# Clusters of 64-wide TensorE work, one pool of PSUM banks, a contiguous q/k copy and weights in pieces, in a fused attention and FFN kernel

## The chip, the cores and the metric

The kernel runs on one core of one Trainium2 chip. The metric is the device time of one execution in microseconds (us), as the median of several runs. A profile is one execution taken with the hardware profiler, so its span differs a little from the median. TensorE appears in the profile as PE (matmuls) and PEld (weight loads), VectorE as DVE, ScalarE as ACT, GpSimd as POOL, SyncE as SP. In this kernel SBUF holds the operands, and TensorE's results go to PSUM, which the program divides into 8 banks, and are copied out from there.

## The reference, cut to what matters

```python
# B=8, heads H=12, S=448, D=64;  F = H*D = 768, FF = 2048
scores = scale * q @ k.T
scores = einsum('bhij,hg->bgij', scores, w_pre)      # mixes the heads
attn   = softmax(scores)
attn   = einsum('bhij,hg->bgij', attn, w_post)       # mixes the heads again
x      = (attn @ v) as [B*S, F]
out    = relu(x @ w_in)**2 @ w_out
```

## The kernel before

The program is written as a list of tasks with dependencies. TensorE runs its tasks in the order in which they are listed. A small planner orders the tasks of the other engines by start time and then by priority (a lower number goes first), and gives each copy out of PSUM to ACT or DVE. So the order of everything is fixed before the run.

One batch has these parts. I use the names in the rest of the text:

- T: transposes of q and k, one pair of heads at a time, into one PSUM bank; copied to SBUF.
- QK: scores of a pair of heads, two matmuls with 64 contraction rows that run side by side in the two row halves of the array; copied into `stage`.
- A DMA on the SP queue copies 10 query rows x 12 heads from `stage` into `dring`, so that heads lie on partitions. This is one *chunk*; a batch has 45.
- pre (head mix by w_pre), exp on ACT, then post (head mix by w_post, 4 matmuls), then a copy into `a2t`.
- AV: attention times v, 64 output columns a head, so two heads side by side in the column halves of the array. It runs once for the first part of a batch's chunks and once for the rest.
- F1 and F2: the two FFN products, with the square (`h2t`) on POOL.

T and AV use the array as two 128x64 halves, QK as two 64x128 halves, the rest as one 128x128 array.

```python
# four fixed pairs of banks: scores, pre, post, everything else
psA = pp("psA", [128, 2, 512], DT.float32)
psP = pp("psP", [128, 2, 512], DT.float32)
psQ = pp("psQ", [128, 2, 512], DT.float32)
psF = pp("psF", [128, 2, 512], DT.float32)
...
def emit_T(b, p):                       # one pair of heads, one task
    ... 16 transposes into one psF bank ...
    def fn_q(eng, en, p=p, pb=pb, bank=bank):          # q: written with a stride
        o = qtp[:, pb, p, :].rearrange("d (j r) -> d r j", r=RJ)
        i_ = psF_bf[:, bank, 0:S].rearrange("d (r j) -> d r j", r=RJ)
        return copy(eng, en, o, i_)
    def fn_k(...): return copy(eng, en, ktp[:, pb, p, :], psF_bf[:, bank, S:2 * S])
    tk = add(..., [t_tr, tq] + war, ...)               # k waits for q
...
def emit_load_w():                      # two loads, each a whole weight
    last["w_in"]  = plan.add("ldwin",  POOL, fn_in,  [qk_tasks[(0, H - 1)]], ..., -300.0, ...)
    last["w_out"] = plan.add("ldwout", POOL, fn_out, [qk_tasks[(0, H - 1)]], ..., -299.0, ...)
# q and k of batch b: priority b * 1000.0 - 500.0
...
head = weave(units_AV(b - 1, 1), late_f2, 2)   # AV units one by one, between other work
body = weave(f1, units_T(b + 1), 2)            # so are the T units
```

The softmax here doesn't subtract the row's maximum and nothing guards it: scores larger than these inputs give would overflow.

Of the kernel before, what the change touches and what calls it, by code (L numbers as in the profile page):

```python
# [8 lines left out]
DT = mybir.dt  # L9
# [8 lines left out]
SEM_LAT = 60.0  # L18
ACT_BIAS = 50.0
# [11 lines left out]
class _Task:  # L31
# [4 lines left out]
                 "end", "order", "nwait", "succs", "clock", "avail")  # L36

    def __init__(self, name, engine, fn, deps, cost, prio, sem, seminc):
        self.name = name
        self.engine = engine  # L40
        self.fn = fn
        self.deps = []
        for d in deps:
            if d is not None and d not in self.deps:
                self.deps.append(d)
        self.cost = cost
        self.prio = prio
        self.sem = sem
        self.seminc = seminc
        self.semval = 0  # L50
        self.end = None
        self.clock = None


class _Plan:
# [11 lines left out]
    def schedule(self):  # L67
# [11 lines left out]
        npe = 0  # L79
        ready = [t for t in self.tasks if t.nwait == 0 and t.engine != PE]  # L80
        while len(committed) < len(self.tasks):
# [16 lines left out]
            if e == PE:  # L98
                npe += 1
            else:  # L100
                ready.remove(t)
# [15 lines left out]
def bass_talking_heads_attention__then__ffn_squared_relu_kernel(  # L117
# [25 lines left out]
    HC = (26, NCH - 26)  # L143
# [4 lines left out]
    with ExitStack() as es:  # L148
# [10 lines left out]
        NH1 = 3  # L159
        ident = sb("ident", [128, 128], DT.bfloat16)  # L160
# [12 lines left out]
        qtp = sb("qtp", [128, 2, NP, S], DT.bfloat16)  # L173
        ktp = sb("ktp", [128, 2, NP, S], DT.bfloat16)
# [9 lines left out]
        psA = pp("psA", [128, 2, 512], DT.float32)  # L184
        psP = pp("psP", [128, 2, 512], DT.float32)
        psQ = pp("psQ", [128, 2, 512], DT.float32)
        psF = pp("psF", [128, 2, 512], DT.float32)
        psF_bf = psF.bitcast(DT.bfloat16)
# [7 lines left out]
        sem_qk = [Sm("dqk%d" % i) for i in range(6)]  # L196
        sem_v = Sm("dv")
        sem_w = [Sm("dwin"), Sm("dwout")]
# [15 lines left out]
        def add(name, engine, fn, deps, cost, prio):  # L214
            return plan.add(name, engine, fn, deps, cost, prio, "ctr", 1)
# [7 lines left out]
        def fn_init(eng, en):  # L223
            eng.memset(ident[:, :], 0.0)
            eng.memset(mask[:, :], 1.0)
            return eng.memset(pring[:, :, S:S + 16], 0.0)

        t_init = add("init", POOL, fn_init, [], {POOL: (800.0, 900.0)}, -1e6)

        def fn_init2(eng, en):  # L230
            eng.affine_select(ident[:, :], ident[:, :], pattern=[[-1, 128]],
                              compare_op=ALU.not_equal, fill=1.0, base=0,
                              channel_multiplier=1)
# [4 lines left out]
        t_init2 = add("init2", POOL, fn_init2, [t_init], {POOL: (800.0, 900.0)}, -1e6 + 1)  # L238

        def fn_init3(eng, en):  # L240
# [4 lines left out]
        t_init3 = add("init3", POOL, fn_init3, [t_init2], {POOL: (400.0, 500.0)}, -1e6 + 2)  # L245
# [16 lines left out]
        t_wk1 = add("wk1", DVE, fn_wk1, [t_wsmall, t_init3], {DVE: (300.0, 400.0)}, -1e6)  # L262
# [7 lines left out]
        t_wk2 = add("wk2", DVE, fn_wk2, [t_wsmall, t_init3], {DVE: (300.0, 400.0)}, -1e6 + 1)  # L270
# [7 lines left out]
        def emit_load_qk(b):  # L278
            step = 2 if b == 0 else H
            for h0 in range(0, H, step):  # L280
                sem = sem_qk[h0 // step]

                def fn(eng, en, b=b, h0=h0, step=step, sem=sem):
# [6 lines left out]
                             {POOL: (2000.0, 5000.0 if b == 0 else 9000.0)}, b * 1000.0 - 500.0, sem, 32)  # L290
# [3 lines left out]
        def emit_load_v(b):  # L294
            def fn(eng, en, b=b):
# [4 lines left out]
                                 {POOL: (1200.0, 8000.0)}, b * 1000.0 - 400.0, sem_v, 16)  # L300

        def emit_load_w():
            def fn_in(eng, en):
                src = bass.AP(moe_w_in.tensor, 0, [[FF, 128], [128 * FF, NFT], [1, FF]])
                eng.dma_start(w_in_sb[:, :, :], src).then_inc(sem_w[0].handle, 16)

            def fn_out(eng, en):
                src = bass.AP(moe_w_out.tensor, 0, [[F, 128], [128 * F, NFFT], [1, F]])
                eng.dma_start(w_out_sb[:, :, :], src).then_inc(sem_w[1].handle, 16)

            last["w_in"] = plan.add("ldwin", POOL, fn_in, [qk_tasks[(0, H - 1)]],
                                    {POOL: (1200.0, 25000.0)}, -300.0, sem_w[0], 16)
            last["w_out"] = plan.add("ldwout", POOL, fn_out, [qk_tasks[(0, H - 1)]],
                                     {POOL: (1200.0, 45000.0)}, -299.0, sem_w[1], 16)


        fbank = {"n": 0, 0: [], 1: []}

        def take_bank():
            i = fbank["n"] % 2  # L320
            fbank["n"] += 1
            return i, fbank[i]
# [4 lines left out]
        def emit_T(b, p):  # L327
            pb = b % 2
            bank, freed = take_bank()

            def fn_tr(eng, en, p=p, bank=bank):
                r_ = None
                for i, src in enumerate((qraw, kraw)):
                    for r in range(RJ):
                        for kk in range(2):
                            r_ = eng.transpose(  # L336
                                psF_bf[kk * 64:kk * 64 + 64, bank,
                                       i * S + r * JB:i * S + (r + 1) * JB],
                                src[:, 2 * p + kk, r, :],
                                ident[0:JB, 0:JB],  # L340
                            )
                return r_

            t_tr = add("tr%d_%d" % (b, p), PE, fn_tr,
                       [qk_tasks[(b, 2 * p)], qk_tasks[(b, 2 * p + 1)], t_init2] + freed,
                       c_mm(2 * RJ, JB, 20.0), 0)
            last["T"] = t_tr

            def fn_q(eng, en, p=p, pb=pb, bank=bank):
                o = qtp[:, pb, p, :].rearrange("d (j r) -> d r j", r=RJ)  # L350
                i_ = psF_bf[:, bank, 0:S].rearrange("d (r j) -> d r j", r=RJ)
                return copy(eng, en, o, i_)

            def fn_k(eng, en, p=p, pb=pb, bank=bank):
                return copy(eng, en, ktp[:, pb, p, :], psF_bf[:, bank, S:2 * S])

            war = [last.get(("qk", b - 2))]
            tq = add("tq%d_%d" % (b, p), FLEX, fn_q, [t_tr] + war, c_ev(S), b * 1000.0 - 700)
            tk = add("tk%d_%d" % (b, p), FLEX, fn_k, [t_tr, tq] + war, c_ev(S),
                     b * 1000.0 - 699)  # L360
            trev[(b, p)] = [tq, tk]
            fbank[bank] = [tq, tk]
# [3 lines left out]
        psA_free = []  # L366

        def emit_QK(b, T, p):
            pb = b % 2
            nr = min(IT, S - T * IT)  # L370
            sl = (b * NIT + T) % 2

            def fn_qk(eng, en, T=T, p=p, pb=pb, nr=nr):
                r_ = None
                for par in range(2):
                    r0 = par * 64
                    r_ = eng.matmul(  # L377
                        psA[0:nr, par, 0:S],
                        qtp[r0:r0 + 64, pb, p, T * IT:T * IT + nr],
                        ktp[r0:r0 + 64, pb, p, 0:S],  # L380
                        start=True, stop=True,
                    )
                return r_

            t_qk = add("qk%d_%d_%d" % (b, T, p), PE, fn_qk, trev[(b, p)] + psA_free,
                       c_mm(1, S, 8.0), 0)
            last[("qk", b)] = t_qk

            def fn_sev(eng, en, p=p, sl=sl, nr=nr):
                return copy(eng, en, stage[0:nr, sl, 2 * p:2 * p + 2, :], psA[0:nr, 0:2, 0:S])  # L390

            t_sev = add("sev%d_%d_%d" % (b, T, p), FLEX, fn_sev,
                        [t_qk] + stage_reader.get(sl, []), c_ev(2 * S),
                        b * 1000.0 + 20 + 10 * T)
            psA_free[:] = [t_sev]
            sev.setdefault((b, T), []).append(t_sev)
            if p == NP - 1:
# [8 lines left out]
        def emit_rel(b, T, u, sl):  # L406
# [5 lines left out]
            def fn(eng, en, u=u, nv=nv, sl=sl, slot=slot):  # L412
# [6 lines left out]
                         {SP: (1200.0, 3200.0)}, g * 1.0, sem_dsl[slot], 16)  # L419
# [19 lines left out]
        def emit_pre(g):  # L439
            b, c = divmod(g, NCH)  # L440
            slot, bank, ps = g % NDS, g % 2, g % NPS

            def fn_pre(eng, en, slot=slot, bank=bank):
                return eng.matmul(psP[0:NR, bank, 0:S], wk1[:, :, :], dring[:, slot, :],  # L444
                                  start=True, stop=True)

            t_pre = add("pre%d_%d" % (b, c), PE, fn_pre,
                        [rel[g], t_wk1, exp_of.get(g - 2)], c_mm(1, S), 0)
# [4 lines left out]
            def fn_exp(eng, en, ps=ps, bank=bank):  # L453
                return eng.activation(pring[:, ps, 0:S], psP[0:NR, bank, 0:S], AF.Exp,  # L454
                                      accum_out=rowsum[:, ps, :])
# [4 lines left out]
            exp_of[g] = t_exp  # L460

            def fn_rec(eng, en, ps=ps):
                return eng.reciprocal(rinv[:, ps, :], rowsum[:, ps, :])  # L463
# [4 lines left out]
            def fn_fold(eng, en, ps=ps, ws=g % NWS):  # L468
# [440 lines left out]
```

## Time and profile before

The median of the first three runs was 715.93 us, and the profiled execution spans 718.5 us.

| what | value | view |
|---|---|---|
| PE busy | 629.5 us, 88% | page, part 1 |
| chain of waits through PE / DMA | 81% / 7% | page, part 4 |
| first post of batch 1 | 144.5 us | timeline |
| batches 2 to 6, first post to first post | 79.9 and 74.1 us in turn, mean 77.6 | timeline |
| PE idle before T of batch 1 | 21.3 us | waits |

The page of the kernel before, its busy shares and two rows of its 40 slices of 18 us (a digit is tenths busy):

```profile
PE 629.5 (88%) x5576; PEld 368.6 (51%) x5576; DVE 380.7 (53%) x946; ACT 488.9 (68%) x1129; POOL 287.0 (40%) x566
PE   3314779987889999999999999999999999999996
PEclk9999799998999999999999999999999999999999
```

There are two stages. For about the first 145 us PE is often idle; after that it is nearly always busy. They have to be read apart.

Waits of PE in the first 146 us of the kernel before (who waited for whom: us in total, times, longest):

```profile
PE psF L336 <- DMA kraw<-in_k_dram: 26.9, 2, 21.3
PE psP L444 <- DMA dring<-stage: 13.0, 7, 5.9
PE psA L377 <- ACT ktp L219: 10.9, 6, 1.8
PE psA L377 <- ACT stage L219: 7.9, 6, 3.0
```

L336 is T, L444 pre, L377 QK. The largest single wait is T of batch 1, which waits for its k. In the timeline of the kernel before it stands in front of all other work of PE:

```profile
41.13 0.63 PE L444 MATMUL psP<-dring,wk 120*120 120x448 bf16 x1 [0.92 <-DMA dring<-stage]
63.08 0.59 PE L336 MATMUL psF<-ident,qraw 112*64 112x112 bf16 x8 [21.32 <-DMA kraw<-in_k_dram]
```

The steady stage of the kernel before, in two batches (window, its length, then busy time of each engine, granted clock, DMA share, GB/s):

```profile
208.00:288.00 80.00, 78.24 (x691) 44.12 (x687) 45.54 (x110) 62.27 (x142) 36.16 (x68) 1.00 0.52 105
288.00:362.00 74.00, 73.89 (x669) 41.52 (x665) 45.37 (x111) 60.61 (x140) 36.15 (x68) 1.00 0.57 109
```

The columns after the length are PE, PEld, DVE, ACT and POOL. PE is busy about 98% of the time or more, so nothing but less PE time helps here. Part of that busy time is not streaming, though. PE's timeline of the kernel before (start, length, instruction, count):

```profile
308.17 0.74 PE L562 MATMUL psF<-xt,w_in_sb 128*128 128x448 bf16 x3
308.84 0.40 PE L377 MATMUL psA<-ktp,qtp 64*120 64x448 bf16 x2
309.17 0.38 PE L489 MATMUL psQ<-wk2s,pring 120*128 120x120 bf16 x4
309.39 0.35 PE L444 MATMUL psP<-dring,wk 120*120 120x448 bf16 x1
309.59 0.73 PE L562 MATMUL psF<-xt,w_in_sb 128*128 128x448 bf16 x3
310.16 0.37 PE L489 MATMUL psQ<-wk2s,pring 120*128 120x120 bf16 x4
310.46 0.39 PE L336 MATMUL psF<-ident,qraw 112*64 112x112 bf16 x8
```

Read the differences of starts, not the lengths, because matmuls overlap. The three F1 matmuls at 309.59 take 0.57 us until the next start, 0.19 each. But the three at 308.17 take 0.67 us, because QK follows them, and the pair of QK takes 0.33 us until post starts, although its 448 columns stream in about 0.19. Over a window of 400 us the medians are 189 ns from F1 to F1, 281 from F1 to QK, and 329 from the last QK matmul to post. I call such a detour to 64-wide work and back an *excursion*. The Trainium skill, "TensorEngine Tiling (Array Packing)", section Tiling Modes (Key Properties), says that a change of tiling mode drains the TensorE. The gaps in this trace fit that (a drain itself is not to be seen in it), and they give the price: one QK pair costs 92 + 3 + 329 = 424 ns, about 235 more than it streams.

### The profile page before, as it was taken

The page shows a single profiled execution, that of the slowest core. Times are in us where ns is not written, and L with a number is a line of the kernel's source. Part 1 is how long each engine was busy: PE and PEld are TensorE (multiplying, and loading weights), DVE is VectorE, ACT ScalarE, POOL GpSimd, SP SyncE. Part 2 cuts the span into 40 slices and gives each one's busy share as a digit, 9 for nine tenths or more (in the row PEclk, how much of TensorE's full clock was granted, in tenths as well). Part 3 has the DMA queues.
Part 4 walks back from the last instruction along what each step waited for, and adds up shares of the span by engine and source line. Part 5 has one row for each costly group of instructions (what it writes and reads, how often), then busy time and mean ns, then how long its engine had stood idle before and what let it go on. Part 6 is the DMA issues. An engine that isn't in the chain of part 4 may idle for free.

```text
span 718.5 us, 14744 instructions
## 1 busy us (share of the span) xinstructions
PE 629.5 (88%) x5576; PEld 368.6 (51%) x5576; DVE 380.7 (53%) x946; ACT 488.9 (68%) x1129; POOL 287.0 (40%) x566
## 2 busy tenths in 40 slices
PE   3314779987889999999999999999999999999996
PEld 1103346554555555555555455555555455557663
DVE  1112564776765645577556455575556554436442
ACT  4314660897878967788778867887788676866510
POOL 6100325343525632357236622565246423742200
PEclk9999799998999999999999999999999999999999
DMA  9994841274656473467445824638463234533011
GB/s 115 215 223 63 131 103 32 61 150 103 100 104 133 80 147 81 110 112 113 106 110 106 135 62 114 130 77 131 117 121 85 54 90 94 97 87 77 23 45 45
DMA packets 84873, 73.32 MB, mean 102 GB/s; under 512 B 4932, under 2 KB 82244, under 8 KB 84804
## 3 DMA queue, kind: packets, MB, share of 16 engines
q0 software_dynamic: 37952, 33.82, 27.1%
q1 hardware_dynamic: 46852, 38.56, 24.0%
q8 instruction: 45, 0.74, 0.4%
q14 instruction: 24, 0.20, 0.1%
HBM read 45.62 MB, written 11.01 MB: 79 GB/s over the span
## 4 chain that ended last, share of the span: by engine, by line
PE 81%; DMA 7%; ACT 4%; DVE 4%; POOL 2%; issue 1%; SPq 0%; POOLq 0%
PE psF L625 21%; PE psF L562 20%; PE psQ L489 13%; PE psP L444 9%; PE psA L377 9%; PE psF L521 6%; DMA kraw<-in_k_dram 6%; PE psF L336 4%; DMA dring<-stage 2%; ACT pring L454 1%; DVE a2t L220 1%; ACT stage L219 1%; POOL h2t L597 1%; DVE qtp L220 1%; ACT a2t L219 1%
## 5 line engine op out<-in xcount | busy, mean ns | idle before, releaser
L469 POOL TENSOR_SCALAR wk2s<-wk2b,rinv 120x120 bf16<-120x120 bf16 x360 | 131.0, 365 | 305.2 <-DVE rinv L463 302.3
L454 ACT ACTIVATE pring<-psP 120x448 bf16<-120x448 f32 x360 | 196.1, 546 | 67.3 <-PE psP L444 65.9
L220 DVE CAST a2t<-psQ 112x480 bf16<-112x480 f32 x221 | 144.5, 656 | 99.5 <-PE psQ L489 95.6
L562 PE MATMUL psF<-xt,w_in_sb 128*128 128x448 bf16 (+2 forms) x960 | 187.0, 316 | 5.1 <-DVE ktp L220 3.2
L625 PE MATMUL psF<-w_out_sb,h2t 128*128 128x384 bf16 x896 | 177.2, 325 | 9.0 <-POOL h2t L597 7.4
L219 ACT ACTIVATE stage<-psA 120x896 bf16<-120x896 f32 (+1 forms) x147 | 134.6, 916 | 60.5 <-PE psA L377 57.4
L444 PE MATMUL psP<-dring,wk 120*120 120x448 bf16 x360 | 135.2, 376 | 14.4 <-DMA dring<-stage 13.0
L489 PE MATMUL psQ<-wk2s,pring 120*128 120x120 bf16 x1440 | 140.5, 221 | 0.1
L489 PEld LDWEIGHTS psQ<-wk2s,pring 120*128 120x128 bf16 x1440 | 93.2, 99 | 63.1 <-issue 25.2
L597 POOL TENSOR_TENSOR h2t<-h1t 128x448 bf16<-128x448 bf16 (+2 forms) x128 | 107.3, 839 | 37.0 <-DVE h1t L588 17.6
L625 PEld LDWEIGHTS psF<-w_out_sb,h2t 128*128 128x128 bf16 x896 | 82.0, 98 | 54.1 <-POOL h2t L597 9.3
L562 PEld LDWEIGHTS psF<-xt,w_in_sb 128*128 128x128 bf16 x960 | 84.1, 99 | 47.8 <-DVE ktp L220 5.6
L463 DVE RECIPROCAL rinv<-rowsum 120x1 f32<-120x1 f32 x360 | 56.6, 158 | 90.6 <-ACT pring L454 87.9
L377 PE MATMUL psA<-ktp,qtp 64*120 64x448 bf16 (+1 forms) x384 | 80.5, 416 | 26.3 <-ACT stage L219 13.6
L219 ACT ACTIVATE a2t<-psQ 112x480 bf16<-112x480 f32 x139 | 80.0, 575 | 28.8 <-PE psQ L489 24.9
L454 ACT ACTIVATION_READ_ACCUMULATOR pring<-psP 120x1 f32 x360 | 71.4, 198 | 0.0
L444 PEld LDWEIGHTS psP<-dring,wk 120*120 120x120 bf16 x360 | 49.1, 136 | 39.8 <-DMA dring<-stage 14.0
L377 PEld LDWEIGHTS psA<-ktp,qtp 64*120 64x120 bf16 (+1 forms) x384 | 25.0, 127 | 81.8 <-issue 32.0
L220 DVE CAST stage<-psA 120x896 bf16<-120x896 f32 (+1 forms) x45 | 49.0, 1090 | 29.4 <-PE psA L377 28.1
L521 PE MATMUL psF<-a2t,vraw 112*64 112x260 bf16 (+1 forms) x768 | 53.5, 264 | 1.7 <-DVE a2t L220 0.7
L220 DVE COPY osb<-psF 128x384 f32<-128x384 f32 x54 | 30.1, 557 | 42.0 <-PE psF L625 42.0
L588 DVE TENSOR_SCALAR h1t<-psF 128x448 bf16<-128x448 f32 (+2 forms) x89 | 43.8, 492 | 10.6 <-PE psF L562 9.0
(33 smaller groups left out, 314.1 us busy)
## 6 DMA issues: line engine op xcount, KB each, us to landing
dring<-stage SPq DMA_DIRECT2D x352, 105.0 KB
out_dram<-osb POOLq DMA_DIRECT2D x24, 384.0 KB, 4.5
vraw<-in_v_dram POOLq DMA_DIRECT2D x8, 672.0 KB, 12.3
qraw<-in_q_dram POOLq DMA_DIRECT2D x7, 672.0 KB, 8.5
kraw<-in_k_dram POOLq DMA_DIRECT2D x7, 672.0 KB, 14.2
w_in_sb<-in_moe_w_in_dram POOLq DMA_DIRECT2D x1, 3072.0 KB, 20.9
w_out_sb<-in_moe_w_out_dram POOLq DMA_DIRECT2D x1, 3072.0 KB, 40.6
out_dram<-osb POOLq DMA_DIRECT2D x8, 192.0 KB, 3.8
```

The source lines that it names most:

```text
L219: return eng.activation(o, i_, AF.Copy)
L220: return eng.tensor_copy(o, i_)
L377: r_ = eng.matmul(psA[0:nr, par, 0:S], qtp[r0:r0 + 64, pb, p, T * IT:T * IT + nr], ktp[r0:r0 + 64, pb, p, 0:S], start=True, stop=True,)
L444: return eng.matmul(psP[0:NR, bank, 0:S], wk1[:, :, :], dring[:, slot, :], start=True, stop=True)
L454: return eng.activation(pring[:, ps, 0:S], psP[0:NR, bank, 0:S], AF.Exp, accum_out=rowsum[:, ps, :])
L463: return eng.reciprocal(rinv[:, ps, :], rowsum[:, ps, :])
L469: return eng.tensor_scalar(wk2s[:, ws, :], wk2b[:, :, :].rearrange("p a b -> p (a b)"), rinv[:, ps, :], 1.0, op0=ALU.mult, op1=ALU.mult)
L489: r_ = eng.matmul(psQ[0:128, bank, jb * NR:(jb + 1) * NR], pring[:, ps, jb * JB:jb * JB + 128], wk2s[:, ws, :], start=True, stop=True,)
L521: r_ = eng.matmul(psF[kk * 64:kk * 64 + 64, bank, 0:n], vraw[:, 2 * p + kk, r, :], a2t[half][:, r, 2 * p + kk, 0:n], start=(r == 0), stop= ...
L562: r_ = eng.matmul(psF[:, bank, 0:n], w_in_sb[:, ft, t16 * 128:(t16 + 1) * 128], xt[:, ft, c0:c1], start=(ft == 0), stop=(ft == NFT - 1),)
L597: return eng.tensor_tensor(h2t[:, t16, o0:o0 + n], h1t[:, s, 0:n], h1t[:, s, 0:n], ALU.mult)
L625: r_ = eng.matmul(psF[:, bank, 0:FH], h2t[:, t16, col:col + 128], w_out_sb[:, t16, hh * FH:(hh + 1) * FH], start=(t16 == 0), stop=(t16 == ...
```

## The change

The intent is to make fewer excursions by running QK in clusters of two pairs, T in clusters of three and AV of a half batch as one cluster. Clusters need more PSUM banks at one time, so all 8 banks become one pool. Further parts: the rows of q and k stay in the order in which they were loaded, so that the copy is contiguous and does q and k together (the output rows are put right by the output DMA, now two DMAs for most tiles); two head pairs of AV share a bank, which limits a half batch to 256 columns and moves the split from 26 chunks to 23; AV goes between F1 and F2; the weights come in 8 pieces, those of w_in in rows of 512 columns; and T of batch 1 is held back to chunks 14 and 18 of batch 0. Smaller parts are not in the cut below, among them: q and k of batch 0 come in three loads instead of six, the later scores of batch 0 are listed three chunks later, and the planner reckons 100 ns for a change of the tile size. In the diffs, `...` marks a cut, and some lines tell an edit in words or shortened.

```diff
-    HC = (26, NCH - 26)
+    HC = (23, NCH - 23)
-        psA = pp("psA", [128, 2, 512], DT.float32)     # and psP, psQ, psF
+        ps = pp("ps", [128, 8, 512], DT.float32)
+        def take(n=1):                                 # the n adjacent banks free longest
+            runs = [list(range(i, i + n)) for i in range(NB - n + 1)]
+            runs = [r_ for r_ in runs if all(i in bank_age for i in r_)]
+            got = min(runs, key=lambda r_: max(bank_age.index(i) for i in r_))
...
-            def fn_q(...): ...                         # strided
-            def fn_k(...): ...
+                def fn_ev(eng, en, p=p, pb=pb, bank=bank):
+                    return copy(eng, en, qkt[:, pb, p, :, :], ps_bf[:, bank, 0:2 * S])
...
+        NWP = 4
-            last["w_in"] = plan.add("ldwin", POOL, fn_in, [qk_tasks[(0, H - 1)]], ..., -300.0, ...)
+                last["w%d_%d" % (i, j)] = plan.add("ldw%d_%d" % (i, j), POOL, fn, [],
+                    ..., -1400.0 + 300.0 * i + j, sem_w[i][j], 16)
-    # q and k of batch b: b * 1000.0 - 500.0
+    # q and k of batch b: -1e7 + h0 if b == 0 else b * 1000.0 - 1500.0
...
-            return [[(..., (lambda p=p: emit_T(b, p)))] for p in range(NP)]
+            return [Group([(..., (lambda p=p: emit_T(b, (p, p + 1, p + 2))))], "T", sl)
+                    for p, sl in zip((0, 3), slots)]
-            body = weave(f1, ts, 2)
+                ts = units_T(b + 1, (14, 18)) if b == 0 else units_T(b + 1)
+            body = weave(f1, ts, 5)
+        NQ = 2                                         # pairs of heads in a QK cluster
+                at = max([0] + [i + 1 for i, g in enumerate(queue) if g.kind == "F1"])
+                queue[at:at] = [g for g in tail if g.kind == "AV"]     # between F1 and F2
```

## The prediction

> **What bounds the kernel now.** The page's busy row gives PE 88% of the span, ACT 68%, DVE 53%; the chain of waits runs 81% through PE and 7% through DMA. Two different stages:
>
> - Start. In the timeline PE idles 21.3 us (41.8 to 63.1) before the transposes of batch 1: their q and k were issued at 23.5 us but stand in the same DMA queue behind the two weight loads, issued at 14.0 and 14.8 us. Only four pre-mix products run before 63 us. The six transpose/score rounds of batch 0 take 3.3 us each because the two copies of q (1.15 us) and k (0.4 to 0.5 us) run one after the other through two banks. Batch 1's first post-mix starts at 144.5 us, of which I count some 63 us as PE work.
> - Steady state (208 to 596 us, five batches of 77.6 us). The windows view has PE busy 78.3 of 80 us, ACT 62, DVE 46: PE bound. Part is not streaming. Start-to-start in PE's timeline: an F1 matmul takes 189 ns before another F1 but 281 before a score pair (+92); pre 193, but 284 before transposes or AV (+91); a score pair occupies 329 ns before post instead of about 190 (+139); leaving AV or transposes costs about 95. The Trainium skill, "TensorEngine Tiling (Array Packing)", Key Properties, says a change of tiling mode drains the TensorE; these gaps agree.
>
> **What the change does.**
> 1. Clusters: a batch has 24 score, 12 AV and 6 transpose excursions; after it 12, 2 and 2. At 231, 187 and 187 ns: 8.9 us before, 3.5 after: 5.4 us a batch, on the critical path. Over the seven PE-bound batches about 37 us.
> 2. AV goes between F1 and F2: hides the 0.9 to 1.6 us that F2 waits for POOL's h2t, some 1 us a batch, 6 in all.
> 3. q/k copies: 1.155 + 0.384 us (DVE) become one contiguous copy, estimate 0.7 to 1.0. ACT and DVE are not the bound: worth little in steady state, but the opening shrinks from 20 us to about 10. Output goes out in two DMAs a tile: POOL issues of 0.6 us, off the path.
> 4. Weight pieces: by the issue priorities the weights still come before batch 1's q and k in the queue, so those land at about 60 us again (1 KB rows: estimate 97 ns from the 60 ns of 512 B and 134 ns of 1536 B packets, slightly slower than 4 KB rows). But the transposes of batch 1 now stand behind 14 chunks, so those chunks run during the load, paced by the stage-to-dring copies (about 50 GB/s under load, 2 us a chunk). I expect batch 1 to start near 110 us instead of 144; 5 us of that is F2 work moved later.
> 5. The pool of 8 banks removes the score waits on stage evictions (13.6 us at ACT, mostly the start). With ACT near 86% in the shorter batch I allow 1 us a batch of new waits.
>
> **Sum.** 716 - 28 (start) - 37 - 6 + 8 (new waits) - some in batch 1 and the tail = about 647 us; 8 in 10 between 622 and 670.
>
> **What would show it.** Score excursions paired in the timeline, batch spacing 71 to 73 us; the wait of the transposes on kraw under 8 us; h2t waits nearly gone; batch 1's first post-mix near 110 us; PE's share of the span over 90%.
>
> **What would make it wrong.** ACT or late banks bounding the shorter batch (spacing stays over 75 us); dring copies starved by the 1 KB rows; the transposes of batch 1 still blocking at chunk 14; or batch 1's q and k landing earlier than I read, which gives up to 15 us more. Faster by over 2%: 0.97.

## The result

The changed kernel took 653.34 us (652.05 to 659.68, 4 runs) against 716.17 us before (4 runs). The ratio is 0.9139, with a 95% interval of 0.9075 to 0.9203. A ratio here is the mean time of one kernel's fast runs over that of the other's fast runs of the same rounds, so it is not quite the ratio of the medians. The kernel ran again later beside other versions: 655.9 us, ratio 0.9126.

The page of the changed kernel, busy shares and the same two rows (slices of 16 us):

```profile
PE 588.0 (90%) x5576; PEld 375.7 (58%) x5576; DVE 345.8 (53%) x828; ACT 468.3 (72%) x1151; POOL 298.1 (46%) x590
PE   4355589896999999999999999999999999999996
PEclk9999979998999999999999999999999999999999
```

The same 5576 matmuls keep PE busy for 41 us less, and the span is 68 us shorter. Waits of PE in the first 125 us of the changed kernel:

```profile
PE ps L470 <- DMA dring<-stage: 26.3, 15, 7.4
PE ps L366 <- DMA kraw<-in_k_dram: 15.7, 2, 7.9
```

L470 is pre and L366 is T. QK's waits for the copies are gone (0.5 us is left). Of the 15.7 us for kraw, 7.7 is the very first load; the wait of T of batch 1 is down from 21.3 to 7.9 us. It now stands behind the pre products of 19 chunks, where it stood behind 4, as the timeline of the changed kernel shows:

```profile
59.55 0.58 PE L470 MATMUL ps<-dring,wk 120*120 120x448 bf16 x1
68.05 0.58 PE L366 MATMUL ps<-ident,qraw 112*64 112x112 bf16 x8 [7.92 <-DMA kraw<-in_k_dram]
```

Two batches of the steady stage of the changed kernel (columns as before):

```profile
252.60:320.30 67.70, 67.49 (x658) 41.71 (x657) 41.82 (x98) 57.37 (x141) 36.74 (x69) 1.00 0.61 120
320.30:393.00 72.70, 72.70 (x691) 44.95 (x690) 40.90 (x96) 60.51 (x146) 38.35 (x73) 1.00 0.61 119
```

PE is as full as before, in batches that are nearly 7 us shorter. A cluster of two pairs in the changed kernel's timeline:

```profile
330.86 0.82 PE L659 MATMUL ps<-w_out_sb,h2t 128*128 128x384 bf16 x4
331.61 0.59 PE L401 MATMUL ps<-qkt 64*120 64x448 bf16 x4
332.13 0.38 PE L517 MATMUL ps<-wk2s,pring 120*128 120x120 bf16 x4
```

Two pairs now take 0.52 us until post starts, where one pair took 0.33. With the 92 ns on the way in that is 0.61 us, 233 ns more than 2 x 190 of streaming: the same overhead as for one pair, once instead of twice.

Where the 68.2 us of the two spans went, from the first post of each batch:

| part | before | after | gain |
|---|---|---|---|
| start to first post of batch 1 | 144.5 | 118.5 | 25.9 |
| batch 1 | 63.9 | 61.0 | 2.9 |
| batches 2 to 6 (5 batches) | 387.9 | 353.9 | 34.0 |
| batch 7, to the first post of the last chunk | 86.2 | 76.6 | 9.6 |
| after the first post of the last chunk | 36.1 | 40.2 | -4.2 |

The gains are from unrounded times. The medians are only 62.8 us apart: the profiled execution of the kernel before took 720.45 us, more than any of its four timed runs (714.49 to 718.33), so some 4 us of the 68.2 belong to that execution. In batches 2 to 6 the gain is nearly all busy time, as one window over them shows, first before and then after:

```profile
208.36:596.24 387.88, 382.56 (x3383) 215.46 (x3382) 227.72 (x554) 308.19 (x702) 178.90 (x338) 1.00 0.52 105
179.57:533.45 353.88, 353.19 (x3382) 218.20 (x3381) 206.15 (x478) 297.19 (x720) 186.78 (x355) 1.00 0.58 116
```

PE is busy 29.4 us less and idle 4.6 us less (5.3 to 0.7), with the same work.

The last two rows of the table belong together: with the split at chunk 23 one tile of F2 no longer fits into batch 7 and runs in the tail.

The copies of q and k, by shape, first before and then after (count, busy us, mean ns of one):

```profile
L220 DVE COPY qtp<-psF 128x448 bf16<-128x448 bf16 x28 | 32.3, 1155 | 23.8 <-PE psF L336 23.1
L220 DVE COPY ktp<-psF 128x448 bf16<-128x448 bf16 x37 | 14.2, 384 | 13.6 <-ACT qtp L219 13.2
```

```profile
L226 DVE COPY qkt<-ps 128x896 bf16<-128x896 bf16 x32 | 19.6, 619 | 22.6 <-PE ps L366 21.7
L225 ACT ACTIVATE qkt<-ps 128x896 bf16<-128x896 bf16 x16 | 14.7, 918 | 10.3 <-PE ps L366 10.2
```

On DVE a pair took 1155 + 384 ns in two copies; it takes 619 in one.

### The profile page after: what moved, and what is told of

The parts are those of the page before. It is cut to its first block, busy times and chain, and to the rows that moved or that the text cites. A ratio compares the mean times of both kernels' runs of the same rounds, so it can differ in the third digit from the quotient of the medians.

```text
span 650.3 us, 14931 instructions
## 1 busy us (share of the span) xinstructions
PE 588.0 (90%) x5576; PEld 375.7 (58%) x5576; DVE 345.8 (53%) x828; ACT 468.3 (72%) x1151; POOL 298.1 (46%) x590
## 4 chain that ended last, share of the span: by engine, by line
PE 79%; DMA 11%; ACT 3%; SPq 2%; DVE 2%; another core or an unknown queue 1%; POOL 1%; issue 1%; POOLq 0%; DVEq 0%
PE ps L596 21%; PE ps L659 21%; PE ps L517 11%; DMA dring<-stage 10%; PE ps L470 9%; PE ps L401 7%; PE ps L556 6%; PE ps L366 3%; SPq L438 2%; ACT pring L480 1%; DVE stage L226 1%; DMA kraw<-in_k_dram 1%; ACT a2t L225 1%; POOL h2t L631 1%
## 5 line engine op out<-in xcount | busy, mean ns | idle before, releaser
L480 ACT ACTIVATE pring<-ps 120x448 bf16<-120x448 f32 x360 | 194.7, 542 | 73.1 <-PE ps L470 71.3
L596 PE MATMUL ps<-xt,w_in_sb 128*128 128x448 bf16 (+2 forms) x960 | 189.6, 314 | 0.8 <-ACT xt L225 0.7
L659 PE MATMUL ps<-w_out_sb,h2t 128*128 128x384 bf16 x896 | 177.3, 325 | 3.5 <-POOL h2t L631 2.0
L470 PE MATMUL ps<-dring,wk 120*120 120x448 bf16 x360 | 135.1, 375 | 33.7 <-DMA dring<-stage 32.3
L226 DVE CAST a2t<-ps 112x480 bf16<-112x480 f32 x200 | 128.8, 651 | 63.2 <-PE ps L517 62.4
L517 PEld LDWEIGHTS ps<-wk2s,pring 120*128 120x128 bf16 x1440 | 103.0, 100 | 69.2 <-issue 20.4
L517 PE MATMUL ps<-wk2s,pring 120*128 120x120 bf16 x1440 | 140.4, 221 | 1.5 <-DVE stage L226 1.5
L226 DVE CAST stage<-ps 120x896 bf16<-120x896 f32 (+1 forms) x97 | 105.6, 1088 | 43.6 <-PE ps L401 35.8
L596 PEld LDWEIGHTS ps<-xt,w_in_sb 128*128 128x128 bf16 x960 | 86.9, 98 | 36.4 <-ACT xt L225 0.9
L225 ACT ACTIVATE a2t<-ps 112x480 bf16<-112x480 f32 x160 | 91.3, 571 | 18.6 <-PE ps L517 14.1
L470 PEld LDWEIGHTS ps<-dring,wk 120*120 120x120 bf16 x360 | 49.0, 136 | 58.4 <-DMA dring<-stage 36.8
L226 DVE COPY osb<-ps 128x384 f32<-128x384 f32 x51 | 28.4, 556 | 46.7 <-PE ps L659 46.7
```

The costliest lines, as they stand in the source:

```text
L225: return eng.activation(o, i_, AF.Copy)
L226: return eng.tensor_copy(o, i_)
L470: return eng.matmul(ps[0:NR, bank, 0:S], wk1[:, :, :], dring[:, slot, :], start=True, stop=True)
L480: return eng.activation(pring[:, pr, 0:S], ps[0:NR, bank, 0:S], AF.Exp, accum_out=rowsum[:, pr, :])
L517: r_ = eng.matmul(ps[0:128, bank, jb * NR:(jb + 1) * NR], pring[:, pr, jb * JB:jb * JB + 128], wk2s[:, ws, :], start=True, stop=True,)
L596: r_ = eng.matmul(ps[:, bank, 0:n], w_in_sb[:, ft, t16 * 128:(t16 + 1) * 128], xt[:, ft, c0:c1], start=(ft == 0), stop=(ft == NFT - 1),)
```

## The experiments

Twelve runs were made, eleven of other kernels and one of the changed kernel again. All gave correct results. "Spacing" is the mean of batches 2 to 6 from first post to first post.

| run | median us | ratio to before | first post of batch 1 | spacing |
|---|---|---|---|---|
| before | 716.17 | 1 | 144.5 | 77.6 |
| changed | 653.34 | 0.9139 | 118.5 | 70.8 |
| u1_solo | 690.84 | 0.9600 | 123.2 | 76.8 |
| u2_fixed | 758.44 | 1.0553 | 123.5 | 87.7 |
| u3_solo_fixed | 689.87 | 0.9585 | 122.8 | 76.9 |
| u4_strided | 660.94 | 0.9185 | 117.3 | 72.8 |
| v1_noslots | 672.64 | 0.9329 | 134.1 | 70.7 |
| v2_onepiece | 648.74 | 0.8995 | 114.3 | 71.0 |
| v3_qkfirst | 646.25 | 0.8979 | 113.3 | 71.2 |
| v4_best1 | 643.75 | 0.8938 | 108.9 | 71.0 |
| w1_nq3 | 666.12 | 0.9246 | 119.5 | 73.3 |
| w2_best3 | 637.21 | 0.8838 | 103.1 | 70.7 |
| w3_after_again | 655.90 | 0.9126 | 119.3 | 70.7 |
| x1_best3_long | 639.87 | 0.8881 | 106.6 | 70.9 |

Runs whose names share the first letter ran on one chip (u and v on the same chip, w and x on another). Across letters I compare the ratios, because the kernel before had medians of 716.17 to 721.11 us. Their 95% intervals are about 0.004 to 0.008 wide on either side.

### The steady stage: clusters or the pool of banks?

Theory S says that the gain is fewer switches of the tile size. Rival P says that 8 pooled banks free PE from waiting on evictions. Clusters and pool can each be undone alone, which gives a square of four kernels.

**u1_solo**, clusters undone, pool kept:

```diff
-        NQ = 2
+        NQ = 1
-    T: one group of three pairs;  AV: one group of six pairs
+    T and AV: a group for each pair, woven between other work
```

> The changed kernel with the clusters alone undone: score pairs, transpose pairs and AV pairs go one by one between full-array work (191, 48 and 89 excursions over the kernel instead of 96, 17 and 16), pool of 8 banks, copies and loads as changed. Theory S (the steady gain is fewer switches of the tile size): about 5 us more a batch, spacing of full batches from 70.2 to 75 or 76 us, time near 690 us. Rival P (the gain is that 8 pooled banks free TensorE from waiting on evictions): within 8 us of 653.

Measured: 690.84 us and a spacing of 76.8 us. The program makes 191, 48 and 89 excursions. The time falls where theory S put it, and the spacing a little above its 75 or 76. Undoing the clusters takes back 6.0 of the 6.8 us that a batch had gained. Rival P says that this is waiting; the window over batches 2 to 6 of u1_solo shows that it is not:

```profile
181.51:565.62 384.11, 382.38 (x3383) 216.48 (x3381) 193.71 (x464) 315.42 (x734) 185.65 (x353) 1.00 0.54 106
```

PE is idle for 1.7 us of it, against 0.7 in the changed kernel; 29 of the 30 us are busy time.

**u2_fixed**, pool undone, clusters kept:

```diff
+        bank_class = {"qk": [0, 1], "pre": [2, 3], "post": [4, 5], "f": [6, 7]}
-            runs = [r_ for r_ in runs if all(i in bank_age for i in r_)]
+            runs = [r_ for r_ in runs if all(i in bank_age and i in bank_class[cls] for i in r_)]
```

> The changed kernel with the banks split as before (2 for scores, 2 for pre, 2 for post, 2 for the rest), clusters kept. Theory S: the second pair of a score cluster must wait about 1 us for the eviction of the first, so some 12 us a batch are lost and clusters without the pool are worse than the kernel before: over 720 us. Rival P: the pool's own share of the gain comes back, 680 to 700 us.

Measured: 758.44 us, 5.5% slower than the kernel before. The waits of PE between 190 and 710 us of this run, where L403 is QK:

```profile
PE ps L403 <- ACT stage L225: 38.4, 38, 1.0
PE ps L403 <- DVE stage L226: 34.5, 29, 1.2
```

The second pair of a cluster waits about 1.1 us (72.9 us in 67 waits) for the copy of the first to leave its banks. These lines give some 12 us a batch over about six batches; the spacing rose by 16.9, so they explain most of it, not all.

**u3_solo_fixed**, both undone:

> Both undone, clusters and pool; opening, loads and copies as changed. Theory S: the pool is worth little without clusters, so within 10 us of the run with the clusters alone undone, near 695 us, spacing 76 to 78 us. Rival P: 25 us or more above it.

Measured: 689.87 us, within 1 us of u1_solo, with the same spacing. So the pool is worth nothing when pairs go one by one, and it is worth some 100 us when they go in clusters (ratio 1.0553 against 0.9139, times 716.17; the medians differ by 105). Rival P falls as a separate gain; the pool is the condition for the clusters. This is also why a version that takes over only the clusters would have looked like a refutation of the idea.

**w1_nq3**, clusters of three pairs:

```diff
-        NQ = 2
+        NQ = 3
```

> The changed kernel with score clusters of three pairs (6 banks of the 8) instead of two. Theory S: a score excursion costs about 235 ns beyond its streaming whatever its length (425 - 190 for one pair before, 613 - 380 for two pairs after, from start-to-start times), so 4 excursions fewer a batch save 0.9 us, 6 us in all, 647 us. If 8 banks are too few for clusters of three, waits on stage evictions appear ahead of the scores or of pre and the spacing of batches rises by 1 us or more instead.

Measured: 666.12 us against 655.90 for the changed kernel, so 10 us slower instead of 6 faster. The first half of the expectation holds. An undisturbed cluster of three in its timeline:

```profile
406.50 0.78 PE L401 MATMUL ps<-qkt 64*120 64x448 bf16 x6
407.21 0.38 PE L517 MATMUL ps<-wk2s,pring 120*128 120x120 bf16 x4
```

0.71 us plus 0.09 on the way in, less 3 x 0.19 of streaming, leaves 0.23 us: the overhead is again that of one excursion. But new waits eat more than the saving. PE's waits from 180 to 610 us come to about 14 us in w1_nq3 (largest two below), where the second run of the changed kernel has 2.4:

```profile
PE ps L470 <- DMA dring<-stage: 5.4, 3, 2.6
PE ps L401 <- ACT stage L225: 3.5, 4, 1.0
```

A cluster of three takes 6 of the 8 banks, so it waits for evictions; that the copies into dring come later because they need all scores of their rows is my reading. The waits do not add up to the whole of the loss: batches 2 to 6 took 12.9 us longer (366.5 against 353.6) with PE idle for 12.0 us against 0.5, although some 5 us of switches should have been saved, so about 6 us remain unexplained.

**u4_strided**, the copy of q and k undone:

```diff
-                    return copy(eng, en, qkt[:, pb, p, :, :], ps_bf[:, bank, 0:2 * S])
+                    o = qkt[:, pb, p, 0, :].rearrange("d (j r) -> d r j", r=RJ)
+                    i_ = ps_bf[:, bank, 0:S].rearrange("d (r j) -> d r j", r=RJ)
+                    copy(eng, en, o, i_)
+                    return copy(eng, en, qkt[:, pb, p, 1, :], ps_bf[:, bank, S:2 * S])
-    output rows permuted, two DMAs for most tiles
+    output rows in order, one DMA a tile
```

> The changed kernel with the q copy strided as before (q rows back in natural order, k copied apart, output in one DMA a tile), all in one task per pair. ACT and DVE were not the bound by both theories: the opening grows by about 2 us (three rounds), the batches by less than 0.5 us, 655 to 660 us in all. If ACT and DVE had become the bound, 48 pairs x 0.8 us on either would show as 10 us or more.

Measured: 660.94 us, ratio 0.9185 against 0.9126 and 0.9139; the intervals overlap, so by time alone this is unclear. The spacing, 72.8 instead of 70.8 us, shows a small cost of 2 us a batch in the traces, more than the 0.5 expected. The first T and QK rounds took 11.4 us instead of 9.1, as expected, but batch 1 did not start later for it (117.3 against 118.5 us). PE's waits name it: QK and the post behind it wait for `qkt` or, with DVE still at work, for `rinv` (4.5 + 2.0 + 1.5 = 8 us from 177 to 617 us, about 1.3 us a batch). ACT and DVE are not the bound, but with T in one cluster their latency shows up where QK follows soon.

### The opening: order on PE, or the loads?

Theory O says that the gain of the opening comes from running some 17 chunks before PE stands still at T of batch 1. Rival L says that it comes from the loads (pieces, short rows, earlier issue). When T of batch 1 begins in the changed kernel, 19 pre products and 15 posts have run; in the kernel before, 4 pre products.

**v1_noslots**:

```diff
-                ts = units_T(b + 1, (14, 18)) if b == 0 else units_T(b + 1)
+                ts = units_T(b + 1)
```

> The changed kernel with the two groups of transposes of batch 1 no longer held back to chunks 14 and 18 of batch 0. Theory O (the gain of the opening is that some 17 chunks run while q and k of batch 1 are still on their way): TensorE stands at the transposes until about 68 us with only 4 or 5 chunks begun, batch 1 starts some 15 to 25 us later than the 118.5 us of the changed kernel, time near 673 us. Rival L (the gain of the opening comes from the loads: pieces, short rows, earlier issue): under 5 us.

Measured: 672.64 us, batch 1 at 134.1 us, 15.6 us later. The wait that the slots had shortened is back in PE's waits of the first 125 us:

```profile
PE ps L366 <- DMA kraw<-in_k_dram: 29.0, 2, 28.7
```

T begins at 60.6 us here and at 68.0 in the changed kernel. So k lands 7 us *later* in the changed kernel, because the chunks that run meanwhile take DMA time from its load: the trace's packets show the copies into dring at 65 GB/s from 45 to 65 us of the changed kernel, and at 0 from 45 to 60.5 us here. It is still a good exchange. But the slots are not the whole of the opening: without them batch 1 still starts 10.4 us before that of the kernel before (144.5). The first T and QK rounds end 8.8 us sooner (16.8 against 25.6 us); the earlier issue and the pieces bring k only 2.5 us sooner (60.6 against 63.1). How the 10.4 us divide is not shown.

**v2_onepiece**:

```diff
-        NWP = 4
+        NWP = 1
```

> The changed kernel with each weight in one load of long rows as before. Theory O: batch 1's q and k land behind the weights at about 66 to 68 us all the same, and the chunks still get there first, so within 5 us of 653. Rival L: the copies into dring starve behind 4 KB rows and the time rises by 10 us or more.

Measured: 648.74 us, ratio 0.8995 (0.894 to 0.9049), where the changed kernel has 0.9139 and 0.9126 (lowest end 0.9067). Undoing the pieces did not cost anything, and on these numbers it gains over 1%. The direction is the same in the trace: T of batch 1 starts at 64.6 us instead of 68.0 and the first AV at 80.3 instead of 85.6. PE's waits of the first 125 us and the start of T:

```profile
PE ps L470 <- DMA dring<-stage: 31.7, 15, 10.3
64.59 0.39 PE L366 MATMUL ps<-ident,qraw 112*64 112x112 bf16 x8 [0.23 <-DMA kraw<-in_k_dram]
```

The wait for dring rises from 26.3 us, and that for k of batch 1 falls from 7.9 to 0.2. The packets of the trace show the exchange. From 23 to 30.5 us, with both queues at work, w_in in rows of 1024 bytes (as written) moved 158 GB/s and the dring copies 67; with rows of 4096 bytes w_in moved 196 and the dring copies 24. The chunks come later (chunk 8 at 46.8 us instead of 37.4), but the queue drains sooner, and k of batch 1 stands last in that queue. So of rival L the pieces and short rows fall: in this order they were a small loss. The earlier issue was not undone alone; in v1_noslots it and the pieces together brought k 2.5 us sooner than in the kernel before. Theory O accounts for the largest single part, 15.6 of the 25.9 us.

**v3_qkfirst**, q and k of batch 1 ahead of the weights:

```diff
-                    "ldw%d_%d" % (i, j), POOL, fn, [],
-                    ..., -1400.0 + 300.0 * i + j,
+                    "ldw%d_%d" % (i, j), POOL, fn, [last["T"]],
+                    ..., -400.0 + 30.0 * i + j,
```

> The changed kernel with q and k of batch 1 ahead of all eight weight pieces in the queue. By the trace of the changed kernel the wait of 7.9 us for kraw at 60 us goes; the copies into dring at about 2 us a chunk still pace batch 0, so 5 to 8 us faster, about 646 us. If the wait only turns into one for the weights or for dring, no change.

Measured: 646.25 us, ratio 0.8979. T of batch 1 starts at 58.7 us without a wait for k, and batch 1 at 113.3, 5.2 us sooner. T itself is 9.4 us earlier, so part of the gain is given back: from T to the first post of batch 1 PE waits 8.6 us for dring, against 5.1 in the changed kernel.

**v4_best1**, as v3_qkfirst, with the four pieces of w_out issued after pre of chunk 16:

> As the run before, and the four pieces of w_out are issued only after the pre product of chunk 16 of batch 0, so that the copies into dring have the DMA engines to themselves between about 46 us and then. If the dring copies under load are what paces batch 0, the first AV moves from 85.6 to about 65 to 70 us and the time to 630 to 640 us. If not, as the run before.

Measured: 643.75 us, the first AV at 73.3 us. Better than v3_qkfirst by about 0.5%, and the intervals overlap; the AV moved 7 us (80.2 to 73.3), less than expected, and the time missed the 630 to 640 us. Between 40 and 45 us the dring copies ran dry for another reason: the trace shows them at 13 GB/s there, and PE waits 4.37 us for chunk 12. That chunk is the first of the next 120 query rows, whose last scores PE begins only at 38.15 us. After chunk 17 they met w_out and then q and k of batch 2.

**w2_best3**, built on v4_best1, with more of these removed: w_out after pre of chunk 20, q and k of batch 2 only after the first AV of batch 0, and the scores of batch 0 three chunks earlier.

```diff
-        emit_load_w(1)
+                if s + LP == 20:
+                    emit_load_w(1, pre_of[s + LP])
-    qk_slot = ... - (LQ if b else 17)
+    qk_slot = ... - (LQ if b else 20)
-                t = plan.add("ldqk%d_%d" % (b, h0), POOL, fn, [last.get("T")], ...
+                t = plan.add("ldqk%d_%d" % (b, h0), POOL, fn,
+                             [last.get("T"), last.get("AV") if b == 2 else None], ...
```

> The opening made lighter for the dring copies: q and k of batch 1 ahead of the weights, w_out only after the pre product of chunk 20, q and k of batch 2 only after the first AV of batch 0, score clusters of batch 0 three chunks earlier. If the dring copies under load are what paces batch 0, the first AV comes at 62 to 68 us instead of 73.3 (the run with w_out deferred alone) and the time is 630 to 637 us. If F2 then waits for w_out, or the copies of batch 1 collide with q and k of batch 2 instead, it stays near 642.

Measured: 637.21 us, ratio 0.8838, 2.9% below the changed kernel's 655.90, at the upper end of what was expected. The first AV comes at 65.0 us and batch 1 at 103.1. PE's waits of the first 125 us, where L470 is pre:

```profile
PE ps L470 <- DMA dring<-stage: 17.1, 14, 7.6
```

The wait for dring was 26.3 us in the changed kernel, and the one for k of batch 1 is gone. The spacing is unchanged at 70.7 us, so this gain lies before batch 2. This version beats both kernels.

**w3_after_again**, the changed kernel once more:

> The changed kernel itself again, beside the two others on the same chip, so that the run with the weights in one piece each (648.7 us, ratio 0.8995) can be set against it: 0.910 to 0.914 would mean that pieces and short rows cost about 1 per cent, 0.900 that the difference was the chip's.

Measured: 655.90 us and 0.9126. That makes the pieces and short rows cost about 1%.

**x1_best3_long**, w2_best3 with each weight in one load:

```diff
-        NWP = 4
+        NWP = 1
```

> The fastest version so far (ratio 0.8838) with w_in and w_out each in one load again, so w_in in 4 KB rows. In the run of the changed kernel with long rows the dring copies got 12 to 24 GB/s beside w_in instead of 41 to 67, but q and k behind the weights landed 3 us earlier. Here q and k of batch 1 are ahead of the weights, so only the loss should be left: pre of chunk 8 comes 5 to 9 us later than 36.1 us and the time rises by 3 to 8 us. If short rows are worth nothing even here, it stays within 2 us or falls.

Measured: 639.87 us, ratio 0.8881 (0.8799 to 0.8964) against 0.8838 (0.8793 to 0.8883): unclear by time. The trace goes the expected way: chunk 8 at 46.7 us instead of 36.1 (10.6 us later, where 5 to 9 were expected), the first AV at 71.0 instead of 65.0, batch 1 at 106.6 instead of 103.1, with the dring copies at 23 to 24 GB/s beside the 4096-byte rows. So the traces suggest that whether short rows help depends on what PE waits for. When k stands behind the weights, long rows bring it sooner; when it stands ahead of them, short rows let the chunks through. By the times only the first half is shown (v2_onepiece). Pieces and row length were changed together, so what the pieces alone do stays open.

## Why the prediction was right

The total was 647 us predicted and 653.34 measured, inside the range of 622 to 670. Point by point:

1. *Clusters, 5.4 us a batch, about 37 us.* The mechanism is right, and 6.0 us a batch is near the 5.4. The total is matched less closely than it looks: u1_solo lost 37.5 us of median (690.84 - 653.34), but 33 to 34 by the ratios, and in the traces batches 1 to 7 account for 32 us of 38, with 4.7 in the opening and 1.2 in the tail.
2. *AV between F1 and F2, 6 us.* The waits of F2 for h2t fell from 9.0 us in the whole trace before to 3.3 after, 5.7 us. The size fits, but no run isolated the placement of AV, and the cause is not shown: u1_solo, where AV is woven one by one into F2 again, has only 1.7 us of this wait from 181 to 640 us.
3. *q/k copy 0.7 to 1.0 us, opening from 20 us to about 10.* The copy takes 0.62 us on DVE and 0.92 on ACT. The opening, from first T to the end of the last of the first scores, took 20.1 us (5.5 to 25.6) and takes 9.1 (7.7 to 16.8). "Worth little in steady state" was a little too low: u4_strided lost 2 us a batch.
4. *Batch 1 starts near 110 us.* It started at 118.5. The steps behind it were right: the weights did stay ahead of q and k of batch 1, 15 to 19 chunks ran during the load, and the wait for kraw was 7.9 us, just under the 8 given. Two terms were mis-sized. q and k were to land "at about 60 us again" and came at 68, because the chunks' own DMAs slowed the load; v1_noslots, without those chunks, has them at 60.6. And after T the chunks were not quite free to run: of the 26.3 us of dring waits in the opening, 21.2 came before T, where PE would have had to wait for k anyway, and 5.1 between T and the first post of batch 1.
5. *The pool removes the score waits; 1 us a batch of new waits.* The waits of QK for stage evictions are gone, and hardly any new ones came: 2.4 us from 180 to 610 us. So this allowance of 8 us was too high. It made up for most of the 8.5 us by which the opening was too optimistic. That the total is closer than its parts is luck.

Of the profile signs, these held: scores clustered two pairs at a time, the wait for kraw (7.9 us, predicted under 8), PE's share over 90% (588.0 of 650.3, 90.4%) and, just outside, the spacing (predicted 71 to 73, measured 70.8). The waits for h2t fell to 3.3 us and were not quite gone, and batch 1's start missed its mark, as said under 4.

## What to carry to other kernels

When TensorE is the bound, look at differences of matmul starts where the tile size changes: here each detour to the scores cost about 0.23 us whatever its length (one to three pairs), so fewer and longer detours paid, but only as long as there were PSUM banks to hold the whole detour. Judge such a pair of changes together: with the clusters but without the pool the kernel was 5.5% slower than before (u2_fixed). In an opening that loads a lot, order the DMA queue by the first thing that the in-order engine will stop at, and keep what is needed later out of the way of the small copies that feed it.

## What the Trainium skill lacked or had wrong

- "TensorEngine Tiling (Array Packing)", Tiling Modes: it says that a mode change drains the TensorE, and gives no cost. Here it was 92 ns on the way in (189 to 281 ns), and 233 to 235 ns for an excursion of one, two or three pairs of 64x128 matmuls in all.
- The same page, Restrictions and Gotchas (Gotcha 1: PSUM Pressure), says that row tiling increases PSUM pressure. It does not say that the number of banks decides whether clustering pays: clusters of two pairs took 758.44 us with 2 banks for scores and 653.34 with 8 pooled banks (ratios 1.0553 and 0.9139), and with 8 pooled banks clusters of three already lost 10 us.
- "DMA: Bandwidth & Descriptors", Queues, rings and completion order, says that an engine takes turns between queues packet by packet. It does not give what follows for the shares: beside a load with rows of 4096, 1536 and 1024 bytes, the copies with 896-byte rows on the other queue got about 24, 51 and 67 GB/s. The packets that the trace records, one for each row, did not alternate one to one (777 of 1024 bytes to 377 of 896 from 23 to 28 us of the changed kernel). The page's packet is a bundle of several descriptors, so this does not contradict it.
- "TensorE: Matmul & The Clock Gate", Part 1, warns that clock events in a trace can be unreliable. Between 24 and 60 us of the changed kernel a pre matmul lasted 0.58 to 0.63 us, as it did from 80 to 90 us (0.63) where the recorded clock was 0.59, and 0.35 to 0.40 in the steady stage, but the clock that the profile gives for 20 to 60 us is 1.00; the trace's first clock record comes at 71.2 us. The page does not say that the records of an opening can be missing altogether.
